# Exponentials of a state-space kernel: the first ones moved ahead of a square root, half of them computed as products of two factors

## The chip, the cores and the metric

The kernel runs on one core of a Trainium2 chip. The core has a matrix engine (PE, whose weight loads are shown apart as PEld), a vector engine (DVE), a scalar engine for table functions (ACT), a general engine (POOL, called GpSimd in the code) and a queue engine (SP) that only issues transfers. Each engine runs its own instruction queue in order and waits on semaphores for the others. Matrix results land in PSUM, a small memory that is divided into banks; everything else lives in SBUF (on chip) or DRAM. The metric is the device time of one execution in microseconds (us), as a median over runs.

## The reference

One forward pass and the whole backward pass of a block: `out = x + s * silu(ffn(xn))` with `xn = layernorm(x)`, 2048 tokens of 576 channels. `ffn` is a gated network of width 4608. `s` is a state-space convolution: per channel `d` and state `n` (128 states) it forms

```
dt = exp(log_dt);  logdA = dt * (A_re + i A_im)
P[d,n,l] = exp(logdA[d,n] * l)            # l = 0..2047
K[d,l]   = Re( sum_n C[d,n] * P[d,n,l] * dt[d] * B[d,n] )
y        = causal convolution of xn with K (by FFT) + xn * Dskip
```

The outputs are `out` and the gradients of all twelve inputs that have one. What the change touches is the magnitude of `P`: with `rho = dt * A_re` and `l = 64 a + b`, the kernel needs `exp(rho * b)` for b = 0..63 and `exp(64 * rho * a)` for a = 0..31, for each channel and state: 96 numbers, called E here.

## The kernel before

**Stages.** The program is fully unrolled; a planner orders the instructions of each engine's queue before the run. It simulates the engines, and whenever one is free gives it the ready instruction of the lowest priority number. Inside `prologue` that number is the program order; after it, `self.at(us)` sets it by hand. Where the code says `with self.tc.issue_after(ins):`, the instructions of the block that go to the engine of `ins` are placed behind `ins` in that engine's queue; instructions on other engines are not tied. Tiles come from pools with a fixed number of buffers, and an instruction that writes a tile waits until all users of the buffer's former content are done.

The prologue (the first 130 us or so) does the following, in program order:

- `load_rates` and `load_dvec` load the parameters; `build_selectors` (L347) builds `SELR`, a 128x1536 matrix that holds, for a chunk of 16 channels, the factors b and 64 a at the row of their channel.
- `rho` is split into three bf16 parts (`split3`, L306), written to `PCS_dram` and read back into `LR_` (L259), whose rows are channels: a product of one chunk of `LR_` with `SELR` gives all `rho * b` and `64 rho * a` of 16 channels, states on the partitions.
- `phase1_layernorm` (L143): statistics on DVE, one square root on ACT (L157), the normalised rows `xn_bf` on DVE (L163), and 80 transposes on PE whose results ACT and DVE copy in turn to `xnT` (L174, L176).
- `build_dft_mats` (L538): two 512x512 Fourier matrices `dC` and `dSf`, each by one Sin on ACT (L572, L574), with an Abs between (L573).
- The complex products `Wr`, `Wi` on POOL (L237, L269), their transposes on PE (L276) and 24 scaled copies on ACT (L280) into `WT`.
- `early_exps` (L411): 18 pairs of chunks. Each pair is 6 matmuls of 512 columns into three 1024-column PSUM tiles (L425), three Exp instructions of 1024 columns on ACT (L427) into the tile `E_k` (three buffers), and one write of 768 KB to `E_dram`, issued on SP (L428).
- `early_spectra` (L430): 256 matmuls of 288 columns (L444) with `xn_bf`, `dC` and `dSf`, 32 copies on DVE (L448), 8 writes of 576 KB to `UH_dram` on SP (L450).

PSUM in the prologue: `ex_psu` (the spectra) holds four banks on the right side from the beginning; the transposes of `W` and of the normalised rows hold three on the left; these are closed (`early.close()`) before `ex_ps` (the exponentials) is opened in their place, so no exponential can be started before the transposes have left.

After the prologue, `ffn_hidden` (L740) and `ssm_kernel` (L453) run beside each other: the first multiplies `xnT` by the loaded weights (L757 loads, L773 to L775 matmuls, L777 Silu), the second reads `E_dram` back chunk by chunk (L478) and computes the sines and the sums of `K`. Then come the convolution, the output of the network and the backward pass.

**Queues.** SP issues, in one order that is fixed before the run, the E writes, the spectra writes and then the loads of the network's weights: an E write that is not ready holds up all that stands behind it. POOL issues no transfer in the prologue; later it issues the writes of L787.

Of the kernel before, what the change touches and what calls it, by code (L numbers as in the profile page):

```python
# [61 lines left out]
class K:  # L62
# [23 lines left out]
    def pool(self, **kw):  # L86
        return self.tc.tile_pool(reuse_waits="tile", **kw)
# [55 lines left out]
    def phase1_layernorm(self, sb, small, ps):  # L143
        nc, cfg = self.nc, self.cfg
        L, D, LT, DT = cfg.L, cfg.D, cfg.LT, cfg.DT
        half = D // 2
        nfull = D // P
        rem = D - nfull * P
        xs = self.xs
        mv = sb.tile([P, LT, 2], FP32, name="mv")  # L150
        for i in range(LT):
            stats = small.tile([P, 2, 6], FP32, name="stats")
            nc.vector.bn_stats(stats[:, 0, :], xs[i][:, 0:half])
            nc.vector.bn_stats(stats[:, 1, :], xs[i][:, half:D])
            nc.vector.bn_aggr(mv[:, i, :], stats[:])
        sd = sb.tile([P, LT], FP32, name="sd")
        nc.scalar.activation(out=sd[:], in_=mv[:, :, 1], func=ACT.Sqrt, bias=self.eps_col[:], scale=1.0)  # L157
# [68 lines left out]
    def prologue(self, matp, selp, xp):  # L226
        nc, cfg = self.nc, self.cfg
        D, DT, N, L, LT = cfg.D, cfg.DT, cfg.N, cfg.L, cfg.LT
        aps = self.aps
        pool = self.pool  # L230
        PS = bass.MemoryType.PSUM
# [5 lines left out]
        mul = lambda e, o, a, b: e.tensor_tensor(out=o[:], in0=a[:], in1=b, op=ALU.mult)  # L237
        with pool(name="par_tmp", bufs=1) as tmp, pool(name="sel_tmp", bufs=1) as st, pool(name="ln_sb", bufs=1) as lsb, \
                pool(name="ln_small", bufs=4) as small, pool(name="dftgen", bufs=1) as dg, \
                pool(name="ex_l", bufs=1) as lp, pool(name="ex_e", bufs=3) as ep, pool(name="ex_u", bufs=2) as up, \  # L240
                pool(name="ex_psu", bufs=2, space=PS, side="right") as ups, ExitStack() as late, ExitStack() as early:
            pps = early.enter_context(pool(name="par_ps", bufs=1, space=PS))
            lps = early.enter_context(pool(name="ln_ps", bufs=2, space=PS))
            self.dma_engines = [nc.sync, nc.scalar]
            logdt = self.load_dvec(tmp, aps["A_log_dt"], "logdt", fill=0.0)
            self.load_rates(tmp)
            dskip_col = self.load_dvec(tmp, aps["A_Dskip"], "dskip", fill=0.0)
            SELR = self.build_selectors(st, selp)
# [5 lines left out]
            rho = tmp.tile([P, DT, N], FP32, name="rho")  # L254
# [2 lines left out]
            self.ln_load(lsb)  # L257
            for k in range(3):
                nc.sync.dma_start(out=LR_[k * 16:(k + 1) * 16], in_=self.PCS_dram[2, k].rearrange("(k p) n -> p k n", p=16))  # L259
            self.phase1_layernorm(lsb, small, lps)  # L260
            self.build_dft_mats(matp, dg)
            Wr = tmp.tile([P, DT, N], FP32, name="Wr")
            Wi = tmp.tile([P, DT, N], FP32, name="Wi")
            t1 = tmp.tile([P, DT, N], FP32, name="t1")
# [8 lines left out]
            for src, dsts in ((Wr, ((0, 0, 1.0), (1, 1, -1.0))), (Wi, ((0, 1, -1.0), (1, 0, -1.0)))):  # L273
                for c, (do, dsz) in enumerate(cfg.dch):
                    pt = pps.tile([P, P], FP32, name="pt")
                    nc.tensor.transpose(pt[:, 0:dsz], src[0:dsz, c, :], self.ident_f[0:dsz, 0:dsz])  # L276
                    for (c2, p0, n, h, d1) in self.dsplit():
                        if c2 == c:
                            for (v, r, sc) in dsts:
                                nc.scalar.mul(out=wv[v][:, r, h, d1 // 4:(d1 + n) // 4],  # L280
                                              in_=pt[:, p0:p0 + n].rearrange("p (e d) -> p e d", d=4)[:, :, :, None]
                                              .to_broadcast([P, n // 4, 4, 2]), mul=sc)
            early.close()
            eps = late.enter_context(pool(name="ex_ps", bufs=2, space=PS))
            self.early_exps(SELR, LR_, ep, eps)
            self.early_spectra(up, ups)
            thp = tmp.tile([P, DT, N], FP32, name="thp")
            nc.vector.scalar_tensor_tensor(out=thp[:], in0=self.A_im[:], scalar=1.0 / (2 * PI), in1=dt_b,
                                           op0=ALU.mult, op1=ALU.mult)
            t = tmp.tile([P, DT, N], FP32, name="sr_t")  # L290
            thr = tmp.tile([P, DT, N], FP32, name="thr")
            nc.vector.tensor_scalar(out=t[:], in0=thp[:], scalar1=MAGIC, scalar2=-MAGIC, op0=ALU.add, op1=ALU.add)
            nc.vector.tensor_tensor(out=thr[:], in0=thp[:], in1=t[:], op=ALU.subtract)
            th64 = tmp.tile([P, DT, N], FP32, name="th64")
# [52 lines left out]
    def build_selectors(self, st, selp):  # L347
        nc, cfg = self.nc, self.cfg
        AV, BV, DC = cfg.AV, cfg.BV, 16
        QW, PW = DC * BV, DC * AV  # L350
        self.SEL = selp.tile([P, 2, QW + PW], BF16, name="SEL")
        SELR = st.tile([P, QW + PW], BF16, name="SELR")
        ii = st.tile([P, QW + PW], I32, name="ii")
# [4 lines left out]
                       channel_multiplier=0)  # L358
# [9 lines left out]
        pm = st.tile([P, 1], FP32, name="pm")  # L368
# [22 lines left out]
        return SELR  # L391

    def ssm_forward(self, T0, TK, TC):
        nc, cfg = self.nc, self.cfg
# [13 lines left out]
            self.ssm_kernel(T0, TK, ps, ps1)  # L408
            self.ssm_conv(T0 + TK * NCH, TC, ps, ps1)

    def early_exps(self, SELR, LR_, ep, ps):  # L411
        nc, cfg = self.nc, self.cfg
        D, N = cfg.D, cfg.N
        DC = 16
        NCH = D // DC
        TW = DC * (cfg.AV + cfg.BV)
        self.E_dram = self.dram.tile([NCH, P, TW], BF16, name="E_dram")
        for c2 in range(0, NCH, 2):
            E = ep.tile([P, 2, TW], BF16, name="E_k")
            Ef = E[:].rearrange("p c t -> p (c t)")  # L420
            for o in range(0, 2 * TW, 1024):
                pe = ps.tile([P, 1024], FP32, name="e_ps")
                for k in range(2):
                    ch, o1 = divmod(o + 512 * k, TW)
                    nc.tensor.matmul(pe[:, 512 * k:512 * k + 512], lhsT=LR_[:, c2 + ch, :], rhs=SELR[:, o1:o1 + 512],  # L425
                                     start=True, stop=True)
                nc.scalar.activation(out=Ef[:, o:o + 1024], in_=pe[:], func=ACT.Exp)  # L427
            nc.sync.dma_start(out=self.E_dram[c2:c2 + 2].rearrange("c p t -> p c t"), in_=E[:])  # L428

    def early_spectra(self, up, psu):  # L430
        nc, cfg = self.nc, self.cfg
# [21 lines left out]
    def ssm_kernel(self, T0, TK, ps, ps1):  # L453
# [4 lines left out]
        NCH = D // DC  # L458
        TW = DC * (AV + BV)
        GE = 6  # L460
# [1093 lines left out]
```

## Time and profile before

| | |
|---|---|
| median of 3 runs | 2017.08 us (2015.53 to 2045.22) |
| the profiled execution | 2026.19 us, of which the span of the profile is 2024.4 |
| PE busy | 1785.9 us, 88% of the span |
| DVE, ACT, POOL busy | 1392.8, 888.7, 324.3 us |
| first matmul of the network (L773) | 133.2 us after the start |
| mean granted clock of PE | 0.967 of full speed |

A line of the timeline gives start, duration, engine, code line, operation, `output<-input`, shapes and a count; in brackets stands how long the engine had been idle, and what ended that. "SPq" and "ACTq" are issues of transfers on that queue. Successive instructions of an engine overlap a little, so a steady series is read by the distance between starts.

### The profile page before, as it was taken

How to read it: one execution, taken by the hardware profiler on the slowest of the kernel's cores; microseconds unless marked ns; L12 is line 12 of the kernel's file. 1: busy time of each engine (PE TensorE's matmuls, PEld its weight loads, DVE VectorE, ACT ScalarE, POOL GpSimd, SP SyncE). 2: the span in 40 equal slices, each digit the busy share in tenths (PEclk: the TensorE clock that was granted, in tenths of full speed). 3: DMA queues.
4: the chain of work that ended last, by engine and by line, in shares of the span. 5: the costliest groups of instructions: out<-in, count | busy, mean ns of one | idle time of the engine just before them, and what ended most of it. 6: DMA issues, size and time to landing. Idle time of an engine off the chain costs nothing. (4 is left out here: it accounts for less than half of the span.)

```text
span 2024.4 us, 40373 instructions
## 1 busy us (share of the span) xinstructions
PE 1785.9 (88%) x16465; PEld 1311.4 (65%) x16538; DVE 1392.8 (69%) x2142; ACT 888.7 (44%) x1624; POOL 324.3 (16%) x516
## 2 busy tenths in 40 slices
PE   1789999999999799698989989999899887889977
PEld 0444554445555577577878778887687665667865
DVE  7536565565977255459796596948899844789884
ACT  2867777776554111266464656545444310000000
POOL 5002222221212211101010000111011020231021
PEclk9899999999999899899999999999999998999998
DMA  3588777776655988636565374768999899989995
GB/s 82 193 300 296 250 258 264 263 265 229 221 191 160 281 196 198 186 114 178 167 175 179 116 211 148 197 190 215 223 247 233 192 207 221 218 176 222 234 138 94
DMA packets 624649, 411.25 MB, mean 203 GB/s; under 512 B 427664, under 2 KB 565392, under 8 KB 619856
## 3 DMA queue, kind: packets, MB, share of 16 engines
q1 hardware_dynamic: 565776, 276.34, 56.0%
q0 software_dynamic: 30160, 105.61, 15.5%
q10 hardware_dynamic: 28528, 26.72, 5.0%
q8 instruction: 129, 2.11, 0.4%
q14 instruction: 56, 0.46, 0.1%
HBM read 130.65 MB, written 185.65 MB: 156 GB/s over the span
## 5 line engine op out<-in xcount | busy, mean ns | idle before, releaser
L1417 PEld LDWEIGHTS <-acts 128*128 128x128 bf16 x2304 | 228.4, 100 | 95.6 <-DMA acts<-GG_dram 17.4
L1371 PEld LDWEIGHTS <-xn_bf 128*128 128x128 bf16 x2304 | 224.7, 98 | 34.4 <-issue 8.7
L1036 DVE TENSOR_TENSOR pr_q<-et_ps,pz 128x1024 f32<-128x1024 f32 x144 | 176.1, 1223 | 62.8 <-PE et_ps L1031 54.1
L1322 PE MATMUL ph<-w2T,goT 128*128 128x256 bf16 x1440 | 180.6, 278 | 21.7 <-ACT gh L1325 19.0
L1417 PE MATMUL px<-wT,acts 128*128 128x288 bf16 x1408 | 184.3, 291 | 16.2 <-DMA wT<-in_B_w_dram 16.2
L1039 DVE TENSOR_REDUCE S_all<-pr_q 128x32 f32<-128x1024 f32 x144 | 175.4, 1218 | 3.6
L773 PEld LDWEIGHTS <-xnT 128*128 128x128 bf16 x1152 | 105.3, 98 | 107.7 <-issue 23.4
L1322 PEld LDWEIGHTS <-goT 128*128 128x128 bf16 x1440 | 141.7, 100 | 46.4 <-issue 25.3
L1351 PE MATMUL pgw<-go_o,h_n 128*128 128x288 bf16 x1152 | 155.6, 291 | 10.9 <-ACT gw L1355 8.4
L773 PE MATMUL pg<-wmB_w,xnT 128*128 128x512 bf16 x526 | 158.0, 385 | 5.4 <-ACT g_t L781 2.6
L828 PE MATMUL po<-w2g,hc 128*128 128x288 bf16 x1152 | 147.9, 290 | 13.2 <-DMA w2g<-in_B_w_dram 13.2
L773 PE MATMUL pu<-wmB_w,xnT 128*128 128x512 bf16 x559 | 155.4, 383 | 0.9 <-ACT u_t L782 0.5
L777 ACT ACTIVATE s_t<-pg 128x512 bf16<-128x512 f32 x144 | 86.3, 600 | 148.1 <-PE pu L775 118.0
L828 PEld LDWEIGHTS <-hc 128*128 128x128 bf16 x1152 | 112.7, 99 | 44.8 <-issue 14.6
L1373 ACT CAST gw<-pgw 128x256 bf16<-128x256 f32 x144 | 53.9, 375 | 199.6 <-PE pgw L1371 192.1
L1351 PEld LDWEIGHTS <-h_n 128*128 128x128 bf16 x1152 | 113.9, 99 | 40.5 <-issue 8.6
L1371 PE MATMUL pgw<-gu_n,xn_bf 128*128 128x256 bf16 x1152 | 131.5, 272 | 6.0 <-ACT gw L1355 5.9
L1417 PE MATMUL px<-wA,acts 128*128 128x288 bf16 x896 | 120.1, 294 | 17.1 <-DMA acts<-GG_dram 17.1
L787 POOL DMA_DIRECT2D G_dram<-g_t x72 | 52.4, 728 | 498.9 <-ACT g_t L781 480.1
L1371 PE MATMUL pgw<-gg_n,xn_bf 128*128 128x256 bf16 x1152 | 130.0, 273 | 0.0
L497 ACT ACTIVATE cs_k<-et_ps 128x512 bf16<-128x512 int16 x216 | 116.0, 640 | 6.6 <-PE et_ps L496 6.5
L1325 ACT CAST gh<-ph 128x512 bf16<-128x512 f32 x144 | 81.2, 610 | 81.7 <-PE ph L1322 55.1
(285 smaller groups left out, 3329.9 us busy)
## 6 DMA issues: line engine op xcount, KB each, us to landing
G_dram<-g_t POOLq DMA_DIRECT2D x72, 256.0 KB, 3.3
U_dram<-u_t POOLq DMA_DIRECT2D x72, 256.0 KB, 4.3
H_dram<-h_t SPq DMA_DIRECT2D x72, 256.0 KB, 3.1
Q_dram<-q_k SPq DMA_DIRECT2D x36, 512.0 KB, 3.3
h_n<-U_dram POOLq DMA_DIRECT2D x18, 1024.0 KB, 9.2
gg_n<-G_dram POOLq DMA_DIRECT2D x18, 1024.0 KB, 5.7
GU_dram<-gu_n SPq DMA_DIRECT2D x36, 512.0 KB, 4.7
GG_dram<-gg_n SPq DMA_DIRECT2D x36, 512.0 KB, 6.9
```

The lines of the kernel that those rows point to most:

```text
L497: nc.scalar.activation(out=CS[:, :, o:o + 256], in_=pt[:].bitcast(I16)[:, :, 0::2], func=ACT.Sin, scale=6.283184 / 2 ** 16)
L773: nc.tensor.matmul(pt[:], lhsT=xnT[:, c, ts], rhs=wm[w][:, c, :], start=(c == 0), stop=False)
L777: nc.scalar.activation(out=s_t[:, :, q, :], in_=pgv, func=ACT.Silu)
L828: nc.tensor.matmul(po_[:, pi_, 0:pw], lhsT=hc[:, fi, :], rhs=w2[fi][:, po:po + pw], start=(fi == 0), stop=(fi == FT - 1))
L1036: nc.vector.tensor_tensor(out=pr[:].rearrange("p r k e -> p r (k e)"), in0=T[h][:].rearrange("p k z d a -> p (k z d a)")[:, None].to_broad ...
L1039: nc.vector.tensor_reduce(out=self.S_all[:, :, d0:d0 + 4], in_=pr[:].rearrange("p r k (d a) -> p (r k) d a", d=4), op=ALU.add, axis=AX.X)
L1322: self.pe_last = nc.tensor.matmul(ph[j][:, k, :].rearrange("p (a f) -> p a f", f=P), lhsT=lw, rhs=rh, start=(n == 0), stop=(n == nfull))
L1325: self.sc(lambda: nc.scalar.copy(out=gh[:, j], in_=ph[j][:]))
L1351: self.pe_last = nc.tensor.matmul(pgw[pi_][:, 0:pw], lhsT=hn[:, tt, fl * P:(fl + 1) * P], rhs=go_o[:, tt, po:po + pw], start=(tt == 0), st ...
L1371: self.pe_last = nc.tensor.matmul(pw_[:, 0:FG], lhsT=self.xn_bf[:, tt, c * P:(c + 1) * P], rhs=nat[:, tt, :], start=(tt == 0), stop=(tt == ...
L1373: self.sc(lambda: nc.scalar.copy(out=gw[:, c], in_=pw_[:, 0:FG]))
L1417: self.pe_last = nc.tensor.matmul(px[pi_][:, 0:pw], lhsT=act[:, ai, fi, :], rhs=w[:, po:po + pw], start=(n == 0), stop=(n == len(steps) - 1))
```

## The change

Three things change, all in the prologue.

1. **Banks and order.** The exponentials' PSUM pool (`ex_ps`, four banks) now stands on the right side from the beginning, and the spectra's pool (`ex_psu`) is opened late, in the banks of the transposes. `early_exps` becomes a generator: its first two pairs are emitted before the layer norm, the rest where they were. By two `issue_after` blocks, the ACT instructions of the layer norm and of the Fourier matrices come behind the last Exp of these two pairs, and the 24 copies of `WT` behind the square root.
2. **Products.** Of the 18 pairs, those with `c2 % 4 == 0` (9) are computed as before. For the other 9, only factors are exponentiated: b = 8 i + j gives `exp(8 i rho) * exp(j rho)`, 8 + 8 factors for 64 numbers, and a = 8 i + j in the same way 8 + 4 factors for 32: 28 columns per channel instead of 96, so 2 matmuls of 448 columns and one Exp of 896 columns per pair, in fp32. Four `tensor_tensor` products per pair (1024 and 512 elements for each of two chunks, both inputs read with repeated elements) then write the bf16 tile. The pairs c2 = 6, 18, 30 do them on DVE, the pairs c2 = 2, 10, 14, 22, 26, 34 on POOL. A second selector, `SELF` (128x448), is built by 8 iotas on POOL and 6 DVE instructions.
3. **Space.** Four temporaries of the angles' preparation (`thp`, `sr_t`, `thr`, `th64`) share the buffers of `rho`, `t1`, `Wr` and `Wi`; a new pool `ex_f` holds two factor tiles.

```diff
-        nc.scalar.activation(out=sd[:], in_=mv[:, :, 1], func=ACT.Sqrt, bias=self.eps_col[:], scale=1.0)
+        self.ln_sd = nc.scalar.activation(out=sd[:], in_=mv[:, :, 1], func=ACT.Sqrt, bias=self.eps_col[:], scale=1.0)
...
-                pool(name="ex_psu", bufs=2, space=PS, side="right") as ups, ExitStack() as late, ExitStack() as early:
+                pool(name="ex_f", bufs=2) as fac, \
+                pool(name="ex_ps", bufs=2, space=PS, side="right") as eps, ExitStack() as late, ExitStack() as early:
...
-            self.phase1_layernorm(lsb, small, lps)
-            self.build_dft_mats(matp, dg)
+            exps = self.early_exps(SELR, SELF, LR_, ep, fac, eps)
+            first = [next(exps) for k in range(2)][-1]
+            with self.tc.issue_after(first.ins):
+                self.phase1_layernorm(lsb, small, lps)
+                self.build_dft_mats(matp, dg)
...
+            with self.tc.issue_after(self.ln_sd.ins):
...
             early.close()
-            eps = late.enter_context(pool(name="ex_ps", bufs=2, space=PS))
-            self.early_exps(SELR, LR_, ep, eps)
+            ups = late.enter_context(pool(name="ex_psu", bufs=2, space=PS))
+            for last in exps:
+                pass
             self.early_spectra(up, ups)
-            thp = tmp.tile([P, DT, N], FP32, name="thp")
+            thp = tmp.tile([P, DT, N], FP32, name="thp", tag="rho")
...
+        FW = DC * 28
+        SELF = st.tile([P, FW], BF16, name="SELF")
+        fi = st.tile([P, FW], I32, name="fi")
+        fv = st.tile([P, FW], FP32, name="fv")
+        pd = ([[8, 2], [1, 2], [2, 4]], [[1, DC]])
+        o = 0
+        for (dd, pat) in ((1, [[8, 8]]), (1, [[1, 8]]), (0, [[BV, 2], [8 * BV, 4]]), (0, [[2 * BV, 4]])):
+            n = DC * math.prod(x[1] for x in pat)
+            nc.gpsimd.iota(fi[:, o:o + n], pattern=[[0, DC]] + pat, base=0, channel_multiplier=0)
+            nc.vector.tensor_copy(out=fv[:, o:o + n], in_=fi[:, o:o + n])
+            nc.gpsimd.iota(fi[:, o:o + n], pattern=pd[dd] + [[0, n // DC]], base=0, channel_multiplier=0)
+            o += n
+        fd = fi[:].bitcast(FP32)
+        nc.vector.tensor_copy(out=fd, in_=fi[:])
+        nc.vector.scalar_tensor_tensor(out=SELF[:], in0=fd, scalar=pm[:, 0:1], in1=fv[:], op0=ALU.is_equal, op1=ALU.mult)
...
         for c2 in range(0, NCH, 2):
             E = ep.tile([P, 2, TW], BF16, name="E_k")
+            if c2 % 4 == 0:
...
+            else:
+                FW = DC * 28
+                pe = ps.tile([P, 2, 512], FP32, name="e_ps")
+                F = fac.tile([P, 2, FW], FP32, name="f_k")
+                for ch in range(2):
+                    nc.tensor.matmul(pe[:, ch, 0:FW], lhsT=LR_[:, c2 + ch, :], rhs=SELF[:], start=True, stop=True)
+                last = nc.scalar.activation(out=F[:], in_=pe[:, :, 0:FW], func=ACT.Exp)
+                for ch in range(2):
+                    eng = nc.vector if c2 % 12 == 6 else nc.gpsimd
+                    for (o, w, n1, n0, e0) in ((0, QW, 8, 8, 0), (2 * DC * 8, TW - QW, 8, 4, QW)):
+                        f1 = F[:, ch, o:o + DC * n1].rearrange("p (d x) -> p d x", x=n1)
+                        f0 = F[:, ch, o + DC * n1:o + DC * (n1 + n0)].rearrange("p (d x) -> p d x", x=n0)
+                        eng.tensor_tensor(out=E[:, ch, e0:e0 + w].rearrange("p (d x y) -> p d x y", x=n1, y=n0),
+                                          in0=f1[:, :, :, None].to_broadcast([P, DC, n1, n0]),
+                                          in1=f0[:, :, None, :].to_broadcast([P, DC, n1, n0]), op=ALU.mult)
             nc.sync.dma_start(out=self.E_dram[c2:c2 + 2].rearrange("c p t -> p c t"), in_=E[:])
+            yield last
```

More of the change, by code (lines that the diff above doesn't have):

```diff
@@ L247, in prologue @@
             dskip_col = self.load_dvec(tmp, aps["A_Dskip"], "dskip", fill=0.0)
-            SELR = self.build_selectors(st, selp)
+            SELR, SELF = self.build_selectors(st, selp)
             LR_ = lp.tile([P, D // 16, N], BF16, name="lhs_r")
@@ L272, in prologue @@
             wv = [w[:].rearrange("p c h r d u -> p r h c d u") for w in self.WT]
[L273 to L282, printed above, removed]
+            with self.tc.issue_after(self.ln_sd.ins):
+                for src, dsts in ((Wr, ((0, 0, 1.0), (1, 1, -1.0))), (Wi, ((0, 1, -1.0), (1, 0, -1.0)))):
+                    for c, (do, dsz) in enumerate(cfg.dch):
+                        pt = pps.tile([P, P], FP32, name="pt")
+                        nc.tensor.transpose(pt[:, 0:dsz], src[0:dsz, c, :], self.ident_f[0:dsz, 0:dsz])
+                        for (c2, p0, n, h, d1) in self.dsplit():
+                            if c2 == c:
+                                for (v, r, sc) in dsts:
+                                    nc.scalar.mul(out=wv[v][:, r, h, d1 // 4:(d1 + n) // 4],
+                                                  in_=pt[:, p0:p0 + n].rearrange("p (e d) -> p e d", d=4)[:, :, :, None]
+                                                  .to_broadcast([P, n // 4, 4, 2]), mul=sc)
@@ L289, in prologue @@
                                            op0=ALU.mult, op1=ALU.mult)
-            t = tmp.tile([P, DT, N], FP32, name="sr_t")
-            thr = tmp.tile([P, DT, N], FP32, name="thr")
+            t = tmp.tile([P, DT, N], FP32, name="sr_t", tag="t1")
+            thr = tmp.tile([P, DT, N], FP32, name="thr", tag="Wr")
             nc.vector.tensor_scalar(out=t[:], in0=thp[:], scalar1=MAGIC, scalar2=-MAGIC, op0=ALU.add, op1=ALU.add)
             nc.vector.tensor_tensor(out=thr[:], in0=thp[:], in1=t[:], op=ALU.subtract)
-            th64 = tmp.tile([P, DT, N], FP32, name="th64")
+            th64 = tmp.tile([P, DT, N], FP32, name="th64", tag="Wi")
@@ L390, in build_selectors @@
                                         scalar2=rs[:, 1 - k:2 - k], op0=ALU.mult, op1=ALU.add)
-        return SELR
+        FW = DC * 28
[13 more added lines that the diff above has]
+        nc.vector.scalar_tensor_tensor(out=SELF[:], in0=fd, scalar=pm[:, 0:1], in1=fv[:], op0=ALU.is_equal, op1=ALU.mult)
+        return SELR, SELF
     def ssm_forward(self, T0, TK, TC):
@@ L409, in ssm_forward, with early_exps @@
             self.ssm_conv(T0 + TK * NCH, TC, ps, ps1)
-    def early_exps(self, SELR, LR_, ep, ps):
+    def early_exps(self, SELR, SELF, LR_, ep, fac, ps):
         nc, cfg = self.nc, self.cfg
-        D, N = cfg.D, cfg.N
+        D, N, AV, BV = cfg.D, cfg.N, cfg.AV, cfg.BV
         DC = 16
         NCH = D // DC
-        TW = DC * (cfg.AV + cfg.BV)
+        QW = DC * BV
+        TW = DC * (AV + BV)
         self.E_dram = self.dram.tile([NCH, P, TW], BF16, name="E_dram")
@@ L419, in early_exps @@
             E = ep.tile([P, 2, TW], BF16, name="E_k")
[L420 to L427, printed above, removed]
+            if c2 % 4 == 0:
+                Ef = E[:].rearrange("p c t -> p (c t)")
+                for o in range(0, 2 * TW, 1024):
+                    pe = ps.tile([P, 1024], FP32, name="e_ps")
+                    for k in range(2):
+                        ch, o1 = divmod(o + 512 * k, TW)
+                        nc.tensor.matmul(pe[:, 512 * k:512 * k + 512], lhsT=LR_[:, c2 + ch, :], rhs=SELR[:, o1:o1 + 512],
+                                         start=True, stop=True)
+                    last = nc.scalar.activation(out=Ef[:, o:o + 1024], in_=pe[:], func=ACT.Exp)
+            else:
[13 more added lines that the diff above has]
+                                          in1=f0[:, :, None, :].to_broadcast([P, DC, n1, n0]), op=ALU.mult)
```

## The prediction

> **What bounds the kernel now.** The chain of waits, my first view, is followed back from the end only to 1779 us; it says nothing of the prologue, which is all that the change touches. What a prologue is worth must therefore be read from what starts behind it. From 140 us on PE is nearly always busy (96.31 of the 100 us from 400 to 500 in the view by stretches), so I take a shift of the first network matmul to reach the end one to one, and look for what sets that shift.
>
> The view by stretches (start:end, length; busy us of PE, PEld, DVE, ACT, POOL; clock; DMA share, GB/s):
>
> ```profile
> 60.00:80.00 20.00, 11.18 (x53) 6.17 (x54) 10.84 (x23) 17.85 (x16) 0.00 (x0) 0.66 0.30 92
> 80.00:100.00 20.00, 19.90 (x124) 12.14 (x125) 7.71 (x11) 19.66 (x22) 0.00 (x0) 1.00 0.98 366
> 100.00:120.00 20.00, 19.89 (x123) 11.90 (x123) 7.45 (x10) 19.48 (x22) 0.00 (x0) 1.00 0.91 341
> ```
>
> From 80 to 120 us three things are full at once: PE, ACT and the DMA engines. DVE is half idle and POOL does nothing. Taking work from ACT alone would win nothing; the change takes it from ACT and PE, but not from DMA, as E keeps its size. Before 70 us PE waits for the Fourier matrix. The timeline of ACT around the square root and the Sins:
>
> ```profile
> 40.47 0.45 ACT L280 ACTIVATE WT<-pt 128x128 bf16<-128x128 f32 x2 [0.46 <-PE pt L276]
> 40.93 1.28 ACT L157 ACT_TABLE_LOAD   x1
> 42.23 0.31 ACT L157 ACTIVATE sd<-mv,eps_col 128x16 f32<-128x16 f32 x1
> ...
> 64.09 1.28 ACT L427 ACT_TABLE_LOAD   x1
> 65.38 1.02 ACT L427 ACTIVATE E_k<-e_ps 128x1024 bf16<-128x1024 f32 x1
> 66.42 1.28 ACT L574 ACT_TABLE_LOAD   x1
> 67.72 2.00 ACT L574 ACTIVATE dC<-dft_q,halfpi_col 128x2048 bf16<-128x2048 f32 x1
> ```
>
> The root waits for the WT copies, although the statistics were done at 34.9; and one Exp that slipped between Abs and Sin costs 1.28 + 1.02 + 1.28 = 3.6 us. The end of the stretch:
>
> ```profile
> 123.85 1.49 SPq L450 DMA_DIRECT2D UH_dram<-u_e  x2
> 125.43 1.25 SPq L757 DMA_DIRECT2D wmB_w<-in_B_w_dram  x1
> 128.65 1.42 DVE L448 CAST u_e<-u_ps 128x576 bf16<-128x576 f32 x2 [3.71 <-DMA UH_dram<-u_e]
> 133.19 1.69 PE L773 MATMUL pg<-wmB_w,xnT 128*128 128x512 bf16 x6
> ```
>
> The last E write is issued at about 123.7 (a series of three L428 issues from 117.84, 5.91 long), the first weights behind it at 125.4, and the network starts at 133.2: 9.5 us after the last E write. That distance is my yardstick.
>
> **The change, part by part.**
>
> *First exponentials before the root.* They need `LR_`. Its reads are issued at 27.4 to 28.8 (L259) and take 5.4 us to land by the DMA view, so 34. The selector `SELF` puts six small DVE instructions into the chain before it: four casts of 128 numbers and one of 448 (L363, 0.94 us for 1536, so 0.1 to 0.3 each) and one of L383's kind (1.81 x 448/1536 = 0.5): 1.5 us, if the planner places them there; the eight iotas (0.55 us for 512, L131) fall into POOL's idle 7.2 us before L389. So LR_ at 35.5, the first Exp at 36, three of 1.0 and one of about 0.95: root's table load at 40, root done at 41.6 against 42.5. **Gain 1 us.** This is a new wait: behind these Exps stand the root and everything that needs it, and the root now hangs on a trip through DRAM. Ends: 3 us gained if LR_ comes at 34 without the casts, 2 us lost if the trip takes 3 us more.
>
> *WT copies behind the root.* 24 copies are 11.3 us of queue before the root, 6.4 us busy. ACT idles 10.4 us between the xnT copies (L174), and they fit there; the transposes for them take 10 x 0.45 us of an idle PE. Cost 0 if they fit; without that cover each of the six xnT copies waits up to 0.66 us, 4 us. What is left of the idle time takes three or four more Exps.
>
> *GpSimd beside the normalisation.* The products of pair 2 run at about 40 to 46, beside the `xn_bf` instructions (5.5 us of DVE from 43.5). The timeline of POOL and DVE shows what that does:
>
> ```profile
> 9.46 1.38 POOL L237 TENSOR_TENSOR Wr<-C_re_bf,B_re_bf 128x640 f32<-128x640 bf16 x1
> 9.69 1.18 DVE L209 CAST dskip_f<-dskip_bf 128x5 f32<-128x5 bf16 x1 [4.87 <-DMA dskip_bf<-in_A_Dskip_dram]
> ```
>
> A cast of five columns (0.33 us elsewhere, L209) ends with POOL's instruction. Another cast of 640, L312, took 1.12 instead of 0.48 beside L389, and a two-input L315 took 1.65 instead of 0.77; the L153 statistics ran through POOL's work unchanged at 0.44. So DVE can be held for the rest of a POOL instruction. The Trainium skill (SBUF — State Buffer, "Who interferes with whom") makes this a rule against the change: a DVE instruction with two SBUF inputs and a GpSimd instruction that reads SBUF exclude each other for their whole length, which would hit the DVE products too. The L315 row agrees; by the rule none of the products of both engines overlap. I price from the rows: up to 6 us if every `xn_bf` waits behind pair 2, 0 if POOL finds no turn or is already done; I take 3 and keep both ends. The Fourier matrix comes, with 1 gained and 3 lost, at 69.7 + 2 = 71.7.
>
> *Spectra and exponentials after that.* PE spacing: 0.12 us per 288-column and 0.21 per 512-column matmul at full clock (groups of 2, 3 and 4 in the timeline last 0.41, 0.53, 0.65). Before: 256 x 0.12 + 104 x 0.21 = 53 us of PE after 70. After, with about four of 18 pairs done by then, 7 full pairs (42 x 0.21 = 8.8) and 7 factor pairs (14 x 0.19 = 2.7): 30.7 + 11.5 + 2.5 for the low clock at the start (0.66 above) = 45, so 117. ACT: 21 x 0.97 + 7 x 0.9 = 27 us, no longer a bound. DMA: 14 or 15 pairs of 0.79 MB and 4.7 MB of spectra are 16.5 MB, at 0.37 MB/us 45 us: 117 as well.
>
> *The products.* DVE: 1223 ns for 1024 fp32 elements (L1036), so 2 x (1.22 + 0.61) = 3.7 per pair, 11 us in all in an engine that is half idle. POOL: the nearest row is the product with a repeated input,
>
> ```profile
> L237 POOL TENSOR_TENSOR Wr<-Wr,dt_col 128x640 f32<-128x640 f32 x1 | 1.2, 1246 | 0.0
> L269 POOL TENSOR_TENSOR Wr<-Wr,t 128x640 f32<-128x640 f32 x1 | 1.5, 1528 | 0.0
> ```
>
> 1.95 ns per element, or 2.39 with two full inputs. A pair has 3072: 6.0 or 7.35 us. No row has runs as short as 4 or 8; the farthest row, 128 columns in 664 ns (L303, 5.2 ns), would make 16 us. I take 6.0, the row of the same kind. The skill's GPSIMD Engine Reference ("Engine selection") also advises VectorE for elementwise products, at about half GpSimd's time; by the 4497 ns for 2048 elements of its section 3.1 a pair would be an estimated 6.7 us, inside the bounds of the rows.
>
> Pair 10 can't start before pairs 4, 6 and 8 have left ACT, about 6 us after 71.7: 77.5. Five POOL pairs follow: 30 us. With three E buffers and writes in order, POOL can pause once per two of its pairs for a buffer, a write before it (2.1 us at 0.37 MB/us) and its landing (3.5, DMA view), some 5 us twice; and the eight DVE products of pairs 18 and 30 can be held beside it (L315 lost 0.9 us) or hold it. Ends 0 and 17; I take 8, the middle. So the last E write is issued at 77.5 + 30 + 8 = 115.5, and by the yardstick the network starts at 125, just behind the spectra at 117 to 120. **Gain 8 us.** What is late next is POOL, through SP's order; a stall there holds the weights.
>
> *Shared buffers.* `thp` waits for `rho`, `thr` for the transposes of `Wr`; this chain has until the first sines at 144 us, and costs nothing.
>
> **Sum.** 2026.2 - 8 = 2018 by the profiled execution, which lies 9 us over the median; by the median 2017 - 8 = 2009.
>
> **Rivals.**
>
> - *The products are hidden wholly.* If POOL's last pair ends before the spectra (no pauses, pair 2 without effect on DVE), PE and DMA set the end: spectra done at 115, weights already there, network at 117: gain 16, 2001. For it: DMA and PE are the full ones now. Against it: five pairs of 6 us leave only 10 us of slack from 77.5 to 117.
> - *GpSimd becomes the bound: slower.* The start of the network is 77.5 + 5p + 8 + 9.5; it equals 133.2 at p = 7.6 us per pair, hardly above the row of 7.35. Every us more costs 5. At 12 us the network starts at 155: 2039; at the 16 us of the L303 row 2059. ACT's last Exps and the weights wait in their queues behind it. For it: short runs, exclusion by DVE, and an order planned by estimated durations that can't react. Against it: L237 with its repeated input is the faster of the two rows.
> - *It doesn't do what it says.* LR_ comes late, the root is no earlier, Exps between the Sins cost table loads of 1.28 as at 64.09, and the gain of PE goes there: 2017.
>
> **How the numbers follow.** Forecast (2004 to 2014): 0.42. Hidden wholly: 0.18. GpSimd or the exclusion as bound: 0.28, mostly between 2022 and 2042. No effect: 0.12. The range reaches from 1997 to 2040. A difference of 2% is 40 us here, about what a measurement of this kernel can tell from no change; only the far end of the GpSimd case passes it (0.05), and a gain of 40 would need the prologue at 93 us, less than PE's own work allows (0.01). Within 2%: 0.94.
>
> **What would show it.** The root's ACTIVATE near 41 instead of 42.2; `E_k` products of 1024 on POOL near 2.0 us; DVE's `xn_bf` longer than 0.43 while POOL runs; the first L773 matmul near 125; DMA share still near 1 from 75 to 115. The forecast is wrong if POOL's products take more than 2.4 us, if E's last write is issued after 123.7, or if the planner's order of the later stages moves by itself: an earlier start then doesn't arrive at the end.

## The result and the profile after

The changed kernel takes **2050.26 us in the median of 20 runs (2028.32 to 2069.42)**, the kernel before 2017.19 (20 runs, 2003.09 to 2060.6). The ratio is **1.0141, 95% interval 1.0115 to 1.0167**: some 28 us slower, by the 2% bound "no change", but on the other side of the forecast. The ratio compares undisturbed runs only and is not the quotient of the two medians.

The profiled execution after took 2035.15 us (span 2033.4). The milestones of two profiles of each kernel, in us from the start (each is the start of the instruction, except where it says done):

| | before | before, again | after | after, again |
|---|---|---|---|---|
| first Exp | 65.4 | 65.6 | 40.1 | 40.1 |
| square root | 42.2 | 42.3 | 45.4 | 45.4 |
| first `xn_bf` | 43.5 | 43.6 | 52.7 | 52.7 |
| Fourier matrix `dC` done | 69.7 | 70.0 | 60.7 | 60.7 |
| copies of `WT` | 29.6 to 40.6 | 29.6 to 40.7 | 61.5 to 81.8 | 61.5 to 81.8 |
| spectra on PE, first to last | 69.8 to 132.9 | 70.0 to 133.3 | 82.2 to 151.9 | 82.2 to 152.4 |
| last Exp | 122.3 | 122.7 | 127.5 | 127.1 |
| first matmul of the network | 133.2 | 133.4 | 152.0 | 152.6 |
| first matmul of its output | 671.8 | 672.8 | 687.1 | 686.9 |
| backward weights, first | 862.6 | 864.6 | 876.6 | 875.1 |
| backward weights, last | 1652.2 | 1647.3 | 1672.6 | 1683.5 |
| last matmul begun | 2017.2 | 2003.6 | 2025.9 | 2047.4 |

So 19 us are lost before the network starts, 14 to 15 of them are still there at the network's output, and on the mean of the two profiles another 16 between the first and the last of the backward weights. The table holds both halves of the question.

**Where 19 us went: the view by stretches.** The profile after; columns as in the prediction (stretch, length, busy us of PE, PEld, DVE, ACT, POOL, then clock, DMA share, GB/s):

```profile
60.00:80.00 20.00, 13.69 (x77) 7.73 (x78) 9.68 (x21) 18.18 (x35) 0.00 (x0) 0.67 0.29 97
80.00:100.00 20.00, 16.16 (x80) 9.27 (x80) 18.37 (x18) 8.91 (x13) 14.29 (x8) 0.75 0.55 196
100.00:120.00 20.00, 14.72 (x75) 7.97 (x76) 7.31 (x10) 11.31 (x12) 11.82 (x8) 0.85 0.73 280
120.00:140.00 20.00, 10.75 (x69) 7.08 (x68) 9.22 (x13) 3.88 (x4) 5.91 (x4) 0.81 0.71 270
```

Before, PE had 19.90 and 19.89 of 20 us from 80 to 120, ACT 19.66 and 19.48, and the DMA share was 0.98 and 0.91. Now none of the three is full, and GpSimd is busy 14.29 at most; only DVE comes near, once, with 18.37 from 80 to 100, where its instructions run beside GpSimd's and last longer. No engine is the bound through these 80 us by its work, so the time is lost in waiting. With the gaps the granted clock falls to 0.75 where it was 1.00.

**Who waits: POOL.** The timeline of POOL, profile after, the six pairs:

```profile
44.17 9.48 POOL L463 TENSOR_TENSOR E_k<-f_k 128x1024 bf16<-128x1024 f32 x4 [4.51 <-ACT f_k L457]
...
80.34 7.55 POOL L463 TENSOR_TENSOR E_k<-f_k 128x1024 bf16<-128x1024 f32 x4 [24.09 <-ACT f_k L457]
91.13 6.74 POOL L463 TENSOR_TENSOR E_k<-f_k 128x1024 bf16<-128x1024 f32 x4 [3.24 <-issue]
105.96 5.91 POOL L463 TENSOR_TENSOR E_k<-f_k 128x1024 bf16<-128x1024 f32 x4 [8.09 <-ACT f_k L457]
113.28 5.91 POOL L463 TENSOR_TENSOR E_k<-f_k 128x1024 bf16<-128x1024 f32 x4 [1.42 <-issue]
128.51 5.91 POOL L463 TENSOR_TENSOR E_k<-f_k 128x1024 bf16<-128x1024 f32 x4 [9.32 <-ACT f_k L457]
```

A pair costs 5.91 us undisturbed. From 80.34 to 134.42 POOL works 32.0 us and stands 22.1: it waits for factors that ACT has not made (where the view says "issue", the factors were done within 0.2 us of POOL's start). **ACT** (its timeline, profile after) is not busy either, but waits for the landing of the write that frees one of the three `E_k` buffers:

```profile
84.15 1.94 ACT L450 ACTIVATE E_k<-e_ps 128x1024 bf16<-128x1024 f32 x2 [2.05 <-DMA E_dram<-E_k]
...
108.13 1.94 ACT L450 ACTIVATE E_k<-e_ps 128x1024 bf16<-128x1024 f32 x2 [2.30 <-DMA E_dram<-E_k]
...
115.34 2.85 ACT L450 ACTIVATE E_k<-e_ps 128x1024 bf16<-128x1024 f32 x3 [2.19 <-DMA E_dram<-E_k]
...
123.58 1.94 ACT L450 ACTIVATE E_k<-e_ps 128x1024 bf16<-128x1024 f32 x2 [4.38 <-DMA E_dram<-E_k]
```

**SP** closes the ring (waits of the SP queue, from 0 to 160 us; total, times, longest): the write of a product pair stands in the queue until POOL is done, and all writes of full pairs behind it.

```profile
SPq L466 <- POOL E_k L463: 43.4, 6, 10.0
```

**DVE** (its timeline, profile after) carries the ring to the spectra. A product pair that DVE is to make waits for its factors at the head of DVE's queue, and the copies of spectra that are done stand behind it; later copies wait for the write of an earlier block of spectra:

```profile
119.23 3.57 DVE L463 TENSOR_TENSOR E_k<-f_k 128x1024 bf16<-128x1024 f32 x4 [7.59 <-ACT f_k L457]
122.72 1.42 DVE L487 CAST u_e<-u_ps 128x576 bf16<-128x576 f32 x2
...
139.36 0.76 DVE L487 CAST u_e<-u_ps 128x576 bf16<-128x576 f32 x1 [4.04 <-DMA UH_dram<-u_e]
```

The two spectra copied at 122.72 were finished on PE at 113.1 and 114.5, and both PSUM tiles of the spectra stayed full until then. The write that the copy at 139.36 waits for was issued at 134.90, behind the last E write, which waited for POOL until 134.45: so POOL's last pair sets when the remaining spectra run. **PE** (its timeline, profile after) stands in both places:

```profile
82.15 1.12 PE L483 MATMUL u_ps<-xn_bf,dC 128*128 128x288 bf16 x4 [0.53 <-ACT WT L285]
...
124.65 1.01 PE L448 MATMUL e_ps<-SELR,lhs_r 128*128 128x512 bf16 x2 [4.39 <-ACT E_k L450]
125.46 1.16 PE L483 MATMUL u_ps<-xn_bf,dC 128*128 128x288 bf16 x4
...
140.18 0.65 PE L483 MATMUL u_ps<-xn_bf,dC 128*128 128x288 bf16 x4 [3.66 <-DVE u_e L487]
```

At 124.65 an exponential stands ahead of the spectra in PE's queue, but of its 4.39 us only the last 1.2 held spectra that could have run; before that DVE had not freed a tile. Over the whole prologue such holds by PE's own order come to less than 2 us.

The first line shows a second loss. `dC` was ready at 60.7, 9 us earlier than before, yet the spectra start at 82.15, behind the last `WT` copy: their PSUM pool now lies where the transposes' results are.

**What DVE does while POOL works**, its timeline, profile after:

```profile
43.64 1.22 DVE L607 TENSOR_SCALAR dft_q<-dft_fr 128x2048 f32<-128x2048 f32 x1
44.90 2.85 DVE L608 TENSOR_SCALAR dft_q<-dft_q 128x2048 f32<-128x2048 f32 x1
47.78 3.04 DVE L609 SCALAR_TENSOR_TENSOR dft_fr<-dft_fr,dft_q 128x2048 f32<-128x2048 f32 x1
50.74 0.24 DVE L158 RECIPROCAL rstd<-sd 128x16 f32<-128x16 f32 x1
51.02 1.65 DVE L160 SCALAR_TENSOR_TENSOR negmr<-mv,rstd 128x16 f32<-128x16 f32 x1
52.70 7.45 DVE L163 TENSOR_SCALAR xn_bf<-xt,rstd,negmr 128x576 bf16<-128x576 bf16 x16
```

L607 overlaps pair 2 only in its last 0.7 us and takes 1.22; its twin L608, beside it, 2.85. Without pair 2, in the same order (run e6 below), L608 took 1.23, L609 2.29, L160 0.17 for 2048 numbers, and the 16 `xn_bf` 6.64. The reciprocal, which needs only the root, comes 5.0 us behind it: it stands behind L607 to L609 in DVE's queue, where the kernel before ran their twins after `xn_bf` (L568 at 49.56).

### The profile page after: what moved, and what is told of

It reads as the page before. It is cut to its first block, busy times and chain, and to the rows that moved or that the text cites. A ratio compares the mean times of both kernels' runs of the same rounds, so it can differ in the third digit from the quotient of the medians.

```text
span 2033.4 us, 40334 instructions
## 1 busy us (share of the span) xinstructions
PE 1779.8 (88%) x16431; PEld 1307.2 (64%) x16502; DVE 1419.1 (70%) x2160; ACT 867.4 (43%) x1604; POOL 369.7 (18%) x548
## 3 DMA queue, kind: packets, MB, share of 16 engines
q0 software_dynamic: 30160, 105.61, 15.5%
```

## The experiments

Two theories stood at the start. **A**: the order is at fault; the spectra begin 12 us late, behind the `WT` copies, and this sets the end. **B**: the products are at fault; six pairs that pass through POOL hold the three `E_k` buffers and with them ACT, SP's order and PE's queue. The results, with the first matmul of the network from each profile (133.2 before):

| kernel | ratio to before, 95% interval | network starts |
|---|---|---|
| after | 1.0141 (1.0115 to 1.0167) | 152.0 |
| e1: order alone | 0.9968 (0.9934 to 1.0002) | 131.3 |
| e2: products alone | 1.0083 (1.0031 to 1.0134) | 154.3 |
| e3: all products on DVE | 1.0088 (1.0038 to 1.0137) | 137.1 |
| e13: three POOL pairs for six | 1.0130 (1.0051 to 1.0209) | 144.5 |
| e6: pair 2 in full | 1.0101 (1.0067 to 1.0136) | 146.4 |
| e4: `WT` not tied to the root | 1.0062 (1.0017 to 1.0106) | 153.9 |
| e8: e1, network in other banks | 0.9966 (0.9926 to 1.0006) | 131.9 |
| e10: after, network in other banks | 1.0094 (1.0061 to 1.0126) | 150.7 |
| e11: e8 with two mends | 0.9932 (0.9883 to 0.9981) | 108.7 |
| e12: e11, one pair ahead | 0.9956 (0.9916 to 0.9996) | 112.6 |
| p1, p3: before + 1, 3 memsets | 0.9959 (0.9927 to 0.9991), 0.9990 (0.9951 to 1.0028) | 132.2, 132.6 |
| p2, p4: after + 1, 3 memsets | 1.0145 (1.0097 to 1.0192), 1.0120 (1.0052 to 1.0188) | 152.4, 151.1 |

**The order alone (e1).** All 18 pairs in full on ACT, no `SELF`; banks and order as in the change.

```diff
-            if c2 % 4 == 0:
+            if True:
```

> The order and the banks of the change alone: all 18 pairs in full on ACT, no products, no SELF; the first two pairs (6 Exps) stand before the root, WT copies behind it, the spectra in the banks of the transposes. Theory A (late start: the root waits for LR_, the WT copies hold the spectra's banks): the spectra begin near 80 as in the changed kernel, the first network matmul comes at 145 or later, the time is 20 to 30 us over the kernel before. Theory B (GpSimd pairs in three E buffers hold ACT and, behind it, PE): without products the first network matmul is at 133 or before, the time that of the kernel before or up to 10 us less.

Spectra start at 72.9, behind `WT` copies that end at 72.2, and the network at 131.3, 1.9 us earlier than before; the ratio's interval reaches 1. The order costs nothing, although the spectra wait for the `WT` copies here too. From 80 to 100 us PE is full, as it was before (view by stretches, e1):

```profile
80.00:100.00 20.00, 19.75 (x118) 11.46 (x118) 7.58 (x10) 19.30 (x22) 0.00 (x0) 1.00 0.89 336
```

Theory A falls as the main cause.

**The products alone (e2).** Pools and order as before the change, products as in it.

```diff
-            exps = self.early_exps(SELR, SELF, LR_, ep, fac, eps)
-            first = [next(exps) for k in range(2)][-1]
-            with self.tc.issue_after(first.ins):
-                self.phase1_layernorm(lsb, small, lps)
+            self.phase1_layernorm(lsb, small, lps)
...
-            ups = late.enter_context(pool(name="ex_psu", bufs=2, space=PS))
-            for last in exps:
+            eps = late.enter_context(pool(name="ex_ps", bufs=2, space=PS))
+            for _ in self.early_exps(SELR, SELF, LR_, ep, fac, eps):
```

> The products alone: order and banks of the kernel before, nine pairs as products, six of them on GpSimd. Theory A: the network starts earlier than before, at 122 to 130, and the time falls by 3 to 10 us. Theory B: PE waits behind e_ps as in the changed kernel, the network starts at 140 or later and the time is 10 to 20 us over the kernel before.

Network at 154.3, spectra from 75.3 to 154.1. The same ring as in the change, in its waits of 0 to 160 us (total, times, longest):

```profile
ACT E_k L446 <- DMA E_dram<-E_k: 19.8, 6, 6.3
PE e_ps L444 <- ACT E_k L446: 16.9, 8, 6.8
```

Theory B by itself gives the whole shift of the network, 21.1 us against 18.8 in the change. DVE shows its part here too: two spectra done at 122.4 and 124.3 are copied at 132.8, behind a product pair that waited 7.5 us for its factors.

**Products on DVE (e3).** `eng = nc.vector` for all nine pairs.

> The changed kernel with all nine product pairs on DVE (3.6 us a pair, as measured in it), none on GpSimd. Theory A: GpSimd's share is only its hold on DVE beside the normalisation, so the spectra still begin near 78 to 82 and the network near 145. Theory B: the E buffers come free sooner, the network starts at 138 or before, the time is within 8 us of the kernel before.

Network at 137.1, 15 us earlier than in the change; a DVE pair takes 3.56 us, all nine 32.0. So most of the shift is POOL's. The 3.9 us that are left against the kernel before were not taken apart; in this trace, too, copies of finished spectra stand behind DVE's products (done at 96.9, copied at 99.7). The output's first matmul is at 671.5, as before the change, but the whole is 1.0088: this kernel loses its time after 870 us, like the changed one (below).

**Half of POOL's pairs (e13).** Pairs 10, 22 and 34 in full; POOL keeps 2, 14 and 26.

```diff
-            if c2 % 4 == 0:
+            if c2 not in (2, 6, 14, 18, 26, 30):
```

> The changed kernel with three of the six GpSimd pairs (10, 22, 34) computed in full; pairs 2, 14 and 26 stay on GpSimd, 6, 18 and 30 on DVE. Theory B (each GpSimd pair holds an E buffer for 6 us and more, and ACT and PE behind it): the network begins 7 to 12 us earlier than 152, though ACT and PE have more to do. If the late start of the spectra sets the end, or PE's load does, the network stays at 150 or later.

Network at 144.5, 7.5 earlier than in the change. Each POOL pair taken away is worth 2.5 us at the network, on the mean. PE's waits for ACT's Exps are 14.9 us and ACT's for E writes 13.5, more than the 10.7 and 10.9 of the change, which starts the network later: these two sums are links of the ring, no measure of what it costs. No run gave the ring a fourth E buffer. The whole, 1.013 with a wide interval, can't be told from the change.

**Pair 2 in full (e6).** No POOL product beside the normalisation.

```diff
-            if c2 % 4 == 0:
+            if c2 % 4 == 0 or c2 == 2:
```

> The changed kernel with pair 2 computed in full, so that no product stands beside the normalisation. If GpSimd's hold on DVE there is on the path, xn_bf begins near 45 instead of 52.7 and the network comes 5 to 8 us earlier than 152. If the pairs behind it set the end (theory B), xn_bf begins earlier all the same, but the network stays at 148 or later and the time is within 8 us of the changed kernel's.

The root comes at 47.3 (one Exp more ahead of it), but the first `xn_bf` at 48.9 instead of 52.7, 1.5 behind the root instead of 7.3. The last `WT` copy starts at 77.2, the spectra at 77.5, 4.7 us earlier, the network at 146.4: pair 2 was worth 5.6 us.

**`WT` not tied to the root (e4).** The second `issue_after` is left out.

> The changed kernel without the second ordering block: the WT copies may run before the root again. Theory A: the transposes' banks are free when dC is ready, the spectra begin at 62 to 70 instead of 82 and the network near 140, the time falls by about 10 us against the changed kernel. Theory B: the spectra begin earlier but end behind the GpSimd pairs all the same, network at 148 or later, no gain in time.

`WT` is done at 45, but the root now comes at 63.4, the spectra begin at 83.3 all the same, and the network at 153.9. The reason is a line of ACT's timeline:

```profile
53.85 4.28 ACTq L84 DMA_DIRECT2D PCS_dram<-pc  x6
58.17 1.94 ACT L449 ACTIVATE E_k<-e_ps 128x1024 bf16<-128x1024 f32 x2 [13.01 <-DMA PCS_dram<-pc]
```

Half of `split3`'s writes are issued from ACT's queue. They wait for DVE's data, the planner put six of them ahead of the first Exp, and ACT stood 13.01 us, 4.28 of them while the six were issued. So whether the tie of `WT` costs anything by itself, e4 can't say.

**Banks of the network (e8, e10).** The network's PSUM pool goes to the side of the exponentials, which are done earlier, and no longer waits for the spectra's banks; in e1's kernel (e8) and in the changed one (e10).

```diff
-                    k.pool(name="f_ps", bufs=2, space=bass.MemoryType.PSUM) as fps:
+                    k.pool(name="f_ps", bufs=2, space=bass.MemoryType.PSUM, side="right") as fps:
```

> The order alone (e1_order), and the network's PSUM tiles in the exponentials' banks instead of the spectra's. In e1_order the exponentials left ACT at 110 and the spectra PE at 131, and the network began right behind them. If the banks hold it, its first matmul comes at 118 to 126 and the time is 8 to 15 us below the kernel before; if the order of PE's queue or the weights behind the spectra writes on SP hold it, it stays near 130 and nothing is won over e1_order.

> The changed kernel with the network's PSUM tiles in the exponentials' banks, which come free at 128.5. If the swapped banks hold the network behind the spectra, it begins at 138 to 145 instead of 152 and the time falls by 7 to 14 us; if SP's order (last E write at 134.5, weights behind it) and PE's queue hold it, it begins near 150 and the time stays.

131.9 against 131.3, and 150.7 against 152.0: the banks by themselves do not hold the network. In both kernels its first weights land only some 2 us before it starts (129.5 and 148.9), and the last spectra start at 131.8 and 153.0; whether PE's order or the weights hold it, these two runs do not separate.

**Both kernels again.** One more profile each, no edit.

> The changed kernel once more, for a second profile: the prologue repeats (network at 152 within 1 us), and the later stages show how far one run differs from another. If the gap between 19 us at the network and 28 us at the end is real, some later stage is longer than before in both profiles; if it is scatter, the stages from 670 on differ by some 10 us between the two.

> The kernel before once more, for a second profile: its prologue repeats (network at 133 within 1 us); the stages behind 870 us show whether the changed kernel's longer ones (796 and 808 us from the first to the last backward weight matmul, 790 in the first profile of before) lie outside what one kernel scatters.

They are in the table of milestones. The prologue repeats to 0.6 us, so shifts of several us at the network are real. From the first to the last of the backward weights a kernel's two profiles differ by 7 us (before) and 12 (after).

**Is the loss behind 870 us the planner's doing (p1 to p4)?** After any edit the planner orders all later stages anew. Memsets of one column (0.06 us each) do that and nothing else. Here the theories A and B are others; the text names them.

```diff
         nc.vector.memset(self.halfpi_col[:], PI / 2)
+        pz = const.tile([P, 1], FP32, name="pz")
+        for i in range(1):
+            nc.vector.memset(pz[:, i:i + 1], 0.0)
```

> The kernel before with one memset of one column added behind halfpi_col (0.06 us of an idle VectorE at 0.9 us): the work is the same, but the planner orders all later stages anew. Theory A (the order that the planner happens on is worth several us by itself): the network starts at 133 +- 1 as before, and the whole differs from before by 5 to 15 us to either side. Theory B (the order of the later stages is worth nothing, and the 9 us that the change lost behind the network's start are a consequence of the change): within 0.3%, that is 6 us, of before.

> As the last, with three such memsets, which gives yet another order of the later stages. Theory A: network at 133 +- 1, whole 5 to 15 us off before, and not the same as with one memset. Theory B: within 6 us of before.

> The changed kernel with one memset of one column added. Theory A: network at 152 +- 2, whole between 1.005 and 1.015 of before, as the loss of 19 us at the network is joined by another -10 to +10. Theory B: 1.014 as the changed kernel.

> The changed kernel with three such memsets. Theory A: network at 152 +- 2, whole between 1.005 and 1.015 of before, not the same as with one. Theory B: 1.014.

A new order alone is worth up to 0.41% (p1, 8 us, interval without 1) and 0.1% (p3). But all three orders of the changed kernel lie at 1.012 to 1.0145, so its extra loss is not one unlucky order. The traces show where most of it is. From 1400 to 1500 us PE is busy 76.80 and 68.59 us in the two profiles of the change, 88.58 and 92.37 before: on the mean 18 us less, about the size of the extra loss. PE's longest wait between 1380 and 1500 us was 18.7 and 22.3 us in the change, 18.9 and 19.2 in p2 and p4, 17.4 in e10 (in an execution of 2083.73), 16.0 in e13, 14.7 in e3; it was 8.2 and 3.2 before, 4.4 and 3.1 in p1 and p3, 7.4 in e6, and under 4 in e2 and e4. But it is no mark of the products: of the kernels without any, e1 has 11.5, e8 8.3, e12 (below) 4.8, and e11 (below), whose ratio is the lowest of all, 19.2. Compare the change with e4. From 1407 us to the loads of `wA` near 1437, SP, POOL and ACT issue the same transfers in the same sequence, within 2 us of the same times. But that pair of transposing loads takes twice as long. Timeline of SP and stretches, profile after:

```profile
1438.02 18.00 SPq L1304 DMA_TRANSPOSE wA<-in_B_w_dram  x2
```

```profile
1440.00:1460.00 20.00, 13.73 (x146) 11.85 (x143) 17.29 (x16) 2.98 (x8) 3.17 (x5) 0.97 1.26 134
1460.00:1480.00 20.00, 6.84 (x53) 5.67 (x54) 4.50 (x5) 3.36 (x5) 0.00 (x0) 0.60 1.09 203
```

and the same two views of e4:

```profile
1436.28 9.58 SPq L1303 DMA_TRANSPOSE wA<-in_B_w_dram  x2
```

```profile
1440.00:1460.00 20.00, 18.43 (x192) 15.95 (x190) 19.34 (x19) 5.96 (x12) 3.17 (x5) 1.00 1.10 273
1460.00:1480.00 20.00, 17.74 (x150) 14.54 (x149) 17.39 (x22) 12.95 (x19) 1.65 (x3) 0.91 0.97 207
```

The DMA engines are full in both, but moved 134 GB/s instead of 273, so the loads of the next head (`gz`) land late and PE stands 18.7 us. In e10, e11, e13 and p2 it is another load (`gg_n`) that lands late, so one slow pair is not the whole story. Why the same transfers run at half the speed in some kernels is **open**: it is not the sequence of the issues in the 30 us before, and not the late network, which e2 and e4 have too.

**A better version (e11, e12).** e8 with two mends: `WT` not tied to the root, and, so that ACT is not held as in e4, no more writes issued from ACT in the prologue.

```diff
             self.ln_load(lsb)
+            self.dma_engines = [nc.sync]
```

e12 emits one pair ahead of the layer norm in place of two (`range(1)`).

> The order without the products, mended: all pairs in full, the first two before the root, WT copies not tied to the root, the parts of rho and of the angles written from SP alone (in e4_wt_free ACT stood 13 us behind such an issue), the network's PSUM tiles in the exponentials' banks. If the banks under the transposes are what kept the spectra from their matrix, they begin at 58 to 65 instead of 73, the network at 112 to 122, and the time falls 8 to 18 us below the kernel before. If DMA or PE's queue sets the end all the same, the network stays near 130 and the time within 6 us of the kernel before.

> e11_best with one pair instead of two before the root: three Exps less in front of it. If the Exps in front of the root are on the path, everything behind comes up to 3 us earlier than in e11_best; if not, no difference beyond 1 us at the network.

Spectra from 67.5 and network at 108.7 in e11; 68.1 and 112.6 in e12. These starts of the network, 21 to 25 us earlier than before, can't be set beside the others: its first weights are loaded at 55 to 65 us here, and its first 17 and 19 matmuls run among the spectra, whose last ones start at 126.6 and 126.9, only 6 us earlier than before. At the first matmul of the network's output the two are 15.5 and 17.0 us ahead (656.3 and 654.8). The ratios, 0.9932 and 0.9956, lie below 1, by the 2% bound "no change". Both kernels keep the order of the change without the tie of `WT`, and drop its products. Some 9 to 14 us reach the end, and a gain of 0.4% is what a memset gave by a new order, so how much of it belongs to the prologue is not shown. In e12 the root comes 3.0 us earlier than in e11, at 45.9, but `xn_bf` at 51.4 in both: the Exps ahead of the root are not on the path there.

## Why the prediction was wrong

The forecast was 2009, in a range from 1997 to 2040; the median measured is 2050, about 2045 by the ratio. The rival "GpSimd becomes the bound: slower" had 0.28 and names the right engine, but its condition, a pair of 7.6 us and more, did not come. Step by step:

- **First exponentials before the root** ("LR_ at 35.5", "Gain 1 us"). First Exp at 40.1, root at 45.4 instead of 41.6: a loss of 3.2, over the bound of 2. The six small DVE instructions were priced at 1.5 us undisturbed. In the trace they took 3.0, the one on 448 columns 1.81 instead of 0.5, and the five instructions of the split 7.0 us beside POOL's work, against 4.5 in the kernel before: POOL had made two of its complex products by 12.2 there, and makes all of them from 24.44 on here, beside the split. In e1, which builds no `SELF`, the first Exp comes at 35.6 and the root at 42.8.
- **WT copies behind the root** ("Cost 0 if they fit"). They fitted ACT, but I looked only at the engine. The copies empty PSUM banks that the spectra need now, and the spectra start at 82.2. e1 has the same wait and its network is no later than before. But the wait was not free there either: e11, without the tie (and with two more edits), starts the spectra 5.4 us earlier than e1 and ends them 4.6 us earlier.
- **GpSimd beside the normalisation** (3 us of 0 to 6). `xn_bf` begins 9.2 us later than before, but only part of that is GpSimd's hold. In e6, without pair 2, it begins at 48.9, 3.9 us earlier than in the change, and ends 4.7 earlier; that is the hold, inside the range, and worth 5.6 at the network. The other 5.3 us are the order: L607 to L609 stand ahead of it on DVE, which the prediction did not count, and which also brings the Fourier matrix forward. The Trainium skill (SBUF — State Buffer, "Who interferes with whom") also counts `tensor_scalar` among the instructions that can take the shared ports; the prediction took from it the case of two inputs alone, and L608 (1.23 to 2.85) agrees with the page.
- **Spectra and exponentials after that** ("The Fourier matrix comes ... 71.7", spectra at 117). The matrix came at 60.7, the spectra ended at 151.9. The sum of PE's work was not the mistake; it let the spectra run as if nothing but PE's work held them. They wait for DVE's copies: two finished spectra lay for 8 to 10 us behind a product pair that waited for factors, and later ones for spectra writes behind the last E write. DVE counted as "half idle", which is so, but its queue is in order too.
- **Shared buffers** ("costs nothing"). `thr` waits for the transposes, now until 74.47, as said; but four of its successors on DVE then run beside POOL from 80.74 to 88.24 and take 7.6 us (an L318 2.12 instead of 0.49), and the first spectra copy comes at 88.16 though its spectra were there at 84. Some 4 us by the trace; no run took it alone.
- **The products.** The price was right: 5.91 us a pair against 6.0, DVE 3.56 against 3.7. **The step that failed is "30 + 8": the pauses were 22.1 us, not 8** and over the end of 17, while the start (80.3 for 77.5) and the work (32.0 for 30) were near. I counted a pause "once per two of its pairs for a buffer"; in fact POOL, ACT and SP wait for one another round the ring, and POOL waits longest for factors that ACT can't make while its buffer is in POOL's own write or one that stands behind it. The last E write was issued at 134.45, not 115.5; the prediction's own sign of being wrong was an issue after 123.7.
- **The yardstick** of 9.5 us from the last E write to the network: 17.6 here, since spectra, not weights, were last; they, too, wait for writes behind the E writes in SP's queue.
- **The rival's threshold** (7.6 us per pair) misled: the ring makes POOL the bound at 5.91, as a pair costs its waits and not its work.
- **"Reach the end one to one"** held to within 5 us up to 690 us. Behind 870 it did not: 16 us more in the changed kernel (6 to 26 between the four pairs of profiles), in good part by transfers that landed late around 1440 us, which I could neither foresee nor explain.

## What to carry to other kernels

Before work is moved to a slower engine, follow its output buffer: who else waits for that buffer, in which in-order queues, and what is ready behind them; price the ring of waits, not the instructions alone. When two PSUM pools swap places, look who must leave the banks before the pool that sets the end can use them. A gain below half a per cent in a kernel whose order is planned anew after every edit needs a control that changes only the order.

## What was unexpected in the hardware

GpSimd multiplies two fp32 inputs that repeat in runs of 8 or 4 at 5.91 us per 3072 elements, 1.92 ns each: short runs cost it nothing against L237's 1.95. GpSimd and VectorE slow each other at once: pair 2 took 9.48 us instead of 5.91, and VectorE's L608 2.85 instead of 1.23. A transfer issued from a computing engine's queue holds that engine until its data are there: 13.01 us for six writes in e4. And the same two transposing loads, in the same sequence, took 9.58 us in one kernel and 18.00 in another, with full DMA engines at 273 and 134 GB/s.
